# The last query period of a two-branch attention kernel: normalised and turned in two halves, two output tiles' direct sums started earlier, a late GpSimd unit refused

## The chip, the cores and the metric

One core of one Trainium2 chip runs the kernel. The metric is the device time of one execution in microseconds (us), median of several. The profile is one execution, and its span (first to last instruction) is about 1.8 us shorter than that execution's time.

The **time** and the ratio of times say what a user gets. The **aligned distance** says where it comes from: up to a point shortly before the end all kernels here issue the same work, so I count from the start of the exponential with which ScalarE begins its last 14 sets (823.32 us in the profile of the kernel before, 825.29 in that of the changed one) to an event of the closing sequence. In the expectations of the first four runs the count starts 0.3 us later, at the set of score matmuls where the plans part, so 0.3 has to be added to their figures.

## The reference, cut to what matters

```python
g = sigmoid((x * gate_w).sum(-1, keepdims=True))
a = A_ref(x, A_wqkv, A_wo)      # full attention, 32 heads of 16, 2048 tokens, then @ wo
b = B_ref(x, B_wqkv, B_wo)      # sliding dilated attention, window 8, dilation 2, then @ wo
return g * a + (1 - g) * b
```

Both branches end in a 512x512 output projection. The kernel sums the two projections in one bank of PSUM (the memory that matmuls write to) for each tile of 128 tokens: four row blocks of A's `wo` and four of B's.

## The kernel before

The full attention is cut into 32 periods: 512 queries by 4 heads, 64 score tiles of 128 keys each. The exponential of a tile is done by ScalarE (two or three tiles at a time, through the PSUM "ring"), by VectorE (four passes) or by GpSimd (after a copy by VectorE). A tile that an engine takes is called a unit, and the two or three that ScalarE takes at a time a set. Products with V are added into one PSUM bank, `acc`. A planner in the kernel's Python simulates the engines with fixed durations and so fixes the order of instructions on each engine; the chip then follows that order, waiting on semaphores. After the last period comes the closing sequence, and at the very end a closing barrier, in which all engines meet before the program ends. The parts that the change touches:

```python
# which engine gets a score tile
if psc[0] is not None and rem(p) >= PMIN and P.free_at("psc", now):   # PMIN = 20: GpSimd
    hs = P.take("psc", now)
# ...
# after a period: evict acc, transpose, denominator, reciprocal, normalise
if p == NP - 1:
    st["s"] = work.tile([128, QW], FP32, name="accS", tag="accS", bufs=2)
    yield ("act", -1, 0.40, lambda: A.copy(out=st["s"][:, 0:256], in_=acc[:, 0:256]))
    yield ("dve", 0, 0.42, lambda: V.tensor_copy(out=st["s"][:, 256:QW], in_=acc[:, 256:QW]))
# ...
# last period: turn all four tiles back on the PE, one copy, then one matmul per output tile
def tr(s):
    P.thin = 0.05
    w.open(s, [128, QW], BF16)
    for tt in range(TPC):
        PE.transpose(out=w.t[:, tt * 128:(tt + 1) * 128], in_=otok_tiles[c_][:, cb, tt, :], identity=ident[:])
yield ("pe", 8, 0.37, tr, w.kind)
def cp():
    V.tensor_copy(out=oT_tiles[c_][:, cb, :], in_=w.t[:])
yield ("dve", 8, 0.34, cp)
# ...
# output tiles: 0 and 1 have their sum parked in SBUF, 2 and 3 sum directly in a PSUM bank
def direct_job(tt):
    # ... waits for the other row blocks
    w = Bank("e")                       # banks that are free once the ring is
    # ... seven matmuls of the direct sum
    yield ("wait", ev_ot.setdefault((c_, DC - 1), Event()))
    yield ("pe", tt, MM + SW, lambda: mm(w.t[:], oT_tiles[c_][:, DC - 1, tt * 128:(tt + 1) * 128],
                                         awo[:, DC - 1, :], False, True))
    # ... evicted by ScalarE, stored by ScalarE's queue
```

## Time and profile before

| | before |
|---|---|
| time, median of 3 | 852.29 us (852.24 to 852.29) |
| span of the profile, mean granted clock | 849.9 us, 0.999 |
| ScalarE, VectorE, PE, GpSimd busy | 97%, 90%, 89%, 86% |
| end of the last exponential | 839.40 |
| accumulator closed (end of the last matmul into `acc`) | 840.48 |
| last eviction ends, last store issued | 846.18, 846.21 |
| sync engine wakes as the stores have landed | 848.80 |

A row of the page's groups reads: line, engine, operation, output from input, shapes, count, then busy time and mean, then idle time ahead of it and what ended that. The line is a helper's throughout (L347), so one goes by tile names: `ring` scores, `pT` ScalarE's exponentials, `pd` those of VectorE and GpSimd, `acc` the accumulator, `accS` its copy, `otok` the normalised queries, `oT` the same turned, `osb`/`osc` output tiles. ScalarE bounds the kernel until its last exponential. After that only the closing sequence runs, and every part of the change lies in it or just ahead of it. The lines are shown in the prediction.

### The profile page before, as it was taken

Reading aid. Unit: us, or ns where it says so; the run is one execution under the profiler, and the core shown is the slowest. Engines: PE = TensorE matmul, PEld = TensorE weight load, DVE = VectorE, ACT = ScalarE, POOL = GpSimd, SP = SyncE. Lnnn points to the kernel's source line nnn. Section 1 sums busy time; section 2 is a strip of 40 time slices with the busy share of each in tenths; the row PEclk is TensorE's granted clock in tenths of the full one; section 3 lists DMA queues with packets and bytes.
Section 4 is the critical chain, followed back from the end, with each engine's and each line's share of the span. In section 5 each row is a group of like instructions: output and inputs, shape, how many; then the busy total and the mean of one; then the engine's idle time right before and its main releaser. Section 6 shows DMA issues by size and latency. Waiting matters only on the chain.

```text
span 849.9 us, 15786 instructions
## 1 busy us (share of the span) xinstructions
PE 756.6 (89%) x5867; PEld 267.2 (31%) x5867; DVE 763.3 (90%) x1325; ACT 826.4 (97%) x748; POOL 730.8 (86%) x740
## 2 busy tenths in 40 slices
PE   9999999989998888888998988888898898888886
PEld 4432343333323332323323232332223233223222
DVE  5698889899999899998999899999999999999894
ACT  5999999999999999999999999999999999999995
POOL 2596886999799999899999999999899999987783
PEclk9999999999999999999999999999999999999999
DMA  9002304421345140303122413220313230201000
GB/s 294 6 14 88 99 27 140 152 64 41 127 119 162 34 130 24 112 20 99 41 86 75 137 27 124 67 72 12 101 37 108 87 88 20 62 14 57 14 1 26
DMA packets 72590, 63.85 MB, mean 75 GB/s; under 512 B 20528, under 2 KB 69168, under 8 KB 72512
## 3 DMA queue, kind: packets, MB, share of 16 engines
q1 hardware_dynamic: 71168, 62.44, 24.2%
q8 instruction: 46, 0.75, 0.4%
q10 hardware_dynamic: 1344, 0.39, 0.2%
q14 instruction: 32, 0.26, 0.1%
HBM read 46.14 MB, written 12.62 MB: 69 GB/s over the span
## 4 chain that ended last, share of the span: by engine, by line
ACT 66%; issue 20%; PE 11%; DMA 1%; DVE 1%; SPq 0%; ACTq 0%
ACT pT L347 65%; PE w L347 4%; PE ring L347 3%; PE acc L347 3%; ACT lg L347 1%; DMA xr<-in_A_x_dram 1%; PE e L347 1%; DVE ta L347 0%; PE s L347 0%; SPq L347 0%; DVE pd L347 0%; DVE qpk L347 0%; ACT osc L347 0%; DVE osb L347 0%; DVE kvs L347 0%
## 5 line engine op out<-in xcount | busy, mean ns | idle before, releaser
L347 ACT ACTIVATE pT<-ring 128x1536 bf16<-128x1536 f32 x717 | 816.5, 1408 | 6.7 <-PE ring L347 3.7
L347 PE MATMUL ring<-qt,kt_all 32*128 32x512 bf16 x1841 | 284.9, 380 | 83.1 <-ACT pT L347 70.9
L347 DVE SCALAR_TENSOR_TENSOR ta<-ta,w 128x512 f32<-128x512 f32 x474 | 315.7, 681 | 5.6
L347 POOL TENSOR_TENSOR prod<-prod 128x512 f32<-128x512 f32 (+1 forms) x208 | 240.2, 1166 | 5.5
L347 PE MATMUL acc<-pT,vp_all 128*17 128x512 bf16 x1793 | 221.7, 383 | 1.8 <-DVE accS L347 0.9
L347 PEld LDWEIGHTS <-kt_all 32*128 32x128 bf16 x2096 | 112.8, 91 | 336.3 <-issue 326.2
L347 PE MATMUL acc<-ident,z 128*17 128x512 bf16 (+5 forms) x776 | 198.1, 341 | 1.4 <-POOL ident masks.py:199 1.4
L347 DVE TENSOR_SCALAR ta<-w 128x512 f32<-128x512 uint16 x237 | 161.8, 686 | 36.7 <-PE w L347 34.5
L347 DVE SCALAR_TENSOR_TENSOR pd<-ta,w 128x512 uint16<-128x512 f32 x237 | 159.3, 678 | 2.5
L347 POOL TENSOR_TENSOR prod<-ksh,qb 128x512 f32<-128x512 bf16 x128 | 144.7, 1155 | 2.2
L347 POOL TENSOR_TENSOR prod<-vsh,lg 128x512 f32<-128x512 bf16 x128 | 136.7, 1098 | 3.2 <-DMA vsh<-kv_scr 0.8
L347 PE MATMUL w<-qt,kt_all 32*128 32x512 bf16 x255 | 95.4, 383 | 0.0
L347 PE MATMUL acc<-pd,vp_all 128*17 128x512 bf16 x255 | 83.1, 380 | 0.0
L347 PEld LDWEIGHTS <-z 128*17 128x17 bf16 (+1 forms) x783 | 54.2, 91 | 72.1 <-issue 43.4
L347 PEld LDWEIGHTS <-vp_all 128*17 128x17 bf16 x2048 | 40.7, 87 | 90.8 <-issue 90.3
L347 POOL TENSOR_TENSOR psc<-psc 128x512 f32<-128x512 f32 x54 | 64.4, 1193 | 4.2
L347 PE MATMUL w<-bw,xT 128*128 128x512 bf16 x192 | 49.7, 381 | 0.4
L347 POOL TENSOR_SCALAR psc<-psc 128x512 f32<-128x512 uint16 (+1 forms) x36 | 22.2, 618 | 31.6 <-DVE psc L347 29.1
L347 PEld LDWEIGHTS <-xT 128*128 128x128 bf16 x448 | 31.7, 97 | 28.9 <-issue 16.4
L347 POOL TENSOR_TENSOR lg<-lg,mx 128x256 f32<-128x256 f32 x16 | 10.1, 629 | 21.0 <-DVE mx L347 20.8
L347 DVE COPY accS<-acc 128x512 f32<-128x512 f32 (+1 forms) x32 | 21.6, 674 | 5.3 <-ACT accS L347 5.2
L347 DVE CAST kvs<-w 128x512 bf16<-128x512 f32 x32 | 21.9, 684 | 0.9 <-PE w L347 0.8
(108 smaller groups left out, 453.3 us busy)
## 6 DMA issues: line engine op xcount, KB each, us to landing
ksh<-kv_scr SPq DMA_DIRECT2D x16, 1024.0 KB
vsh<-kv_scr SPq DMA_DIRECT2D x16, 1024.0 KB
kv_scr<-kvs SPq DMA_DIRECT2D x16, 256.0 KB
kt_all<-k_scr SPq DMA_DIRECT2D x6, 512.0 KB
q_scr<-qpk SPq DMA_DIRECT2D x24, 128.0 KB
qt<-q_scr SPq DMA_DIRECT2D x24, 128.0 KB
out_dram<-osb SPq DMA_DIRECT2D x14, 128.0 KB
xr<-in_A_x_dram SPq DMA_DIRECT2D x3, 512.0 KB
```

Of the source, the lines that this page charges most:

```text
L347: return chain_on(self._key, f(*a, **k))
```

## The change

Its intent is to shorten the closing sequence. Cut to its core:

```diff
+    PEND = 32
-            if psc[0] is not None and rem(p) >= PMIN and P.free_at("psc", now):
+            if psc[0] is not None and rem(p) >= (PMIN if p < NP - 1 else PEND) and P.free_at("psc", now):
 ...
         P.spent = True
+        yield ("set", ev_spent)                     # the last score set has been issued
 ...
-            yield ("act", -1, 0.40, lambda: A.copy(out=st["s"][:, 0:256], in_=acc[:, 0:256]))
-            yield ("dve", 0, 0.42, lambda: V.tensor_copy(out=st["s"][:, 256:QW], in_=acc[:, 256:QW]))
+            for hf in range(2):
+                cols = slice(256 * hf, 256 * (hf + 1))
+                yield ("dve", 0, 0.36, lambda: V.tensor_copy(out=st["s"][:, cols], in_=acc[:, cols]))
+                yield ("spawn", last_half(st["s"], hf))
+            return
 ...
+    def last_half(src, hf):    # two tiles: transpose, denominator, reciprocal, normalise, turn back;
+        ...                    # half 0 is copied to oT by ScalarE, half 1 by VectorE
+        yield ("set", ev_last[hf])
 ...  direct_job
-        w = Bank("e")
+        yield ("wait", ev_spent)
+        w = Bank()                                  # the two spare banks, free before the ring is
-        yield ("wait", ev_ot.setdefault((c_, DC - 1), Event()))
+        yield ("wait", ev_last[tt // 2])
 ...
-        yield ("act", 0, 0.06, lambda: A.dma_start(...))
+        if tt < TPC - 1:
+            yield ("spawn", dma_job(lambda: SP.dma_start(...)))   # tile 1 now goes out on sync's queue
+        else:
+            yield ("act", 0, 0.06, lambda: A.dma_start(...))
 ...
-            if c_ == NC - 1 and tt >= 2:            # direct sums: tiles 2 and 3
+            if c_ == NC - 1 and tt % 2 == 1:        # now one in each half: tiles 1 and 3
```

Three parts, then: the **refusal** of the late GpSimd unit, the **early sums**, and the **halves** (with which the choice of tiles and the queue of tile 1's store go).

More of the change, by code (lines that the diff above doesn't have):

```diff
@@ L524 @@
     ev_kdone = Event()
+    ev_spent = Event()
+    ev_last = [Event() for _ in range(2)]
     ev_wq = Event()
@@ L1190, in post_job @@
             st["s"] = work.tile([128, QW], FP32, name="accS", tag="accS", bufs=2)
-            yield ("act", -1, 0.40, lambda: A.copy(out=st["s"][:, 0:256], in_=acc[:, 0:256]))
-            yield ("dve", 0, 0.42, lambda: V.tensor_copy(out=st["s"][:, 256:QW], in_=acc[:, 256:QW]))
-        else:
-            yield ("dve", 0, VP, cp)
+            for hf in range(2):
[3 more added lines that the diff above has]
+            return
+        yield ("dve", 0, VP, cp)
         yield ("set", ev_acc[p + 1])
         yield ("wait", ev_g)
-        w = Bank("e" if p == NP - 1 else "w")
+        w = Bank()
         def tr(s):
@@ L1229, in post_job, with tr, den, nrm @@
             yield ("spawn", ot_job(c_, i // 2))
+    def last_half(src, hf):
+        c_, i = periods[NP - 1]
+        tts = range(2 * hf, 2 * hf + 2)
+        w = Bank("e")
+        st = {}
+        def tr(s):
+            w.open(s, [128, 2, 4, 32])
+            for z, tt in enumerate(tts):
+                PE.transpose(out=w.t[:, z].rearrange("p h d -> p (h d)"), in_=src[:, tt * 128:(tt + 1) * 128],
+                             identity=identf[:])
+        yield ("pe", hf, 0.33, tr, "e")
+        def den():
+            st["r"] = work.tile([128, TPC, 4], FP32, name="rden", tag="rden", bufs=2)
+            db = d1[:, c_ * TPC + 2 * hf:c_ * TPC + 2 * hf + 2]
+            V.tensor_tensor(out=st["r"][:, 0:2], in0=w.t[:, :, :, DH],
+                            in1=_ap(db, [list(db.ap[0]), [1, 2], [0, 4]]), op=ALU.mult)
+        yield ("dve", 1 + hf, 0.11, den)
+        yield ("dve", 1 + hf, 0.14, lambda: V.reciprocal(out=st["r"][:, 0:2], in_=st["r"][:, 0:2]))
+        def nrm():
+            r = st["r"]
+            V.tensor_tensor(out=otok_tiles[c_][:, i // 2, 2 * hf:2 * hf + 2, 64 * (i % 2):64 * (i % 2) + 64]
+                            .rearrange("p t (h d) -> p t h d", d=DH),
+                            in0=w.t[:, :, :, 0:DH], in1=_ap(r[:], [list(r[:].ap[0]), [4, 2], [1, 4], [0, DH]]),
+                            op=ALU.mult)
+        yield ("dve", 1 + hf, 0.24, nrm)
+        yield w.close()
+        w2 = Bank("e")
+        def back(s):
+            P.thin = 0.03
+            w2.open(s, [128, 256], BF16)
+            for z, tt in enumerate(tts):
+                PE.transpose(out=w2.t[:, z * 128:(z + 1) * 128], in_=otok_tiles[c_][:, DC - 1, tt, :],
+                             identity=ident[:])
+        yield ("pe", hf, 0.22, back, "e")
+        dst = oT_tiles[c_][:, DC - 1, 256 * hf:256 * (hf + 1)]
+        if hf == 0:
+            yield ("act", 0, 0.40, lambda: A.copy(out=dst, in_=w2.t[:]))
+        else:
+            yield ("dve", 0, 0.22, lambda: V.tensor_copy(out=dst, in_=w2.t[:]))
+        yield w2.close()
+        yield ("set", ev_last[hf])
     def ot_job(c_, cb):
@@ L1233, in ot_job, with turn @@
             yield ("wait", ev_final[c_ - 2])
-        ev = ev_ot.setdefault((c_, cb), Event())
-        if c_ < NC - 1 or cb < DC - 1:
-            def turn():
-                if c_ not in oT_tiles:
-                    oT_tiles[c_] = work.tile([128, DC, QW], BF16, name="oT", tag="oT", bufs=2)
-                SP.dma_start_transpose(out=oT_tiles[c_][:, cb, :].rearrange("p (t n) -> p t n", n=128),
-                                       in_=otok_tiles[c_][:, cb].rearrange("p t d -> p (t d)"))
-            yield ("sp", 0, 0.1, turn)
-            yield ("delay", TURN)
-            if cb == DC - 1:
-                yield ("set", ev_turned[c_])
-            yield ("set", ev)
-            return
-        w = Bank("e")
-        def tr(s):
-            P.thin = 0.05
-            w.open(s, [128, QW], BF16)
-            for tt in range(TPC):
-                PE.transpose(out=w.t[:, tt * 128:(tt + 1) * 128], in_=otok_tiles[c_][:, cb, tt, :],
-                             identity=ident[:])
-        yield ("pe", 8, 0.37, tr, w.kind)
-        def cp():
-            V.tensor_copy(out=oT_tiles[c_][:, cb, :], in_=w.t[:])
-        yield ("dve", 8, 0.34, cp)
-        yield w.close()
-        yield ("set", ev)
+        def turn():
+            if c_ not in oT_tiles:
+                oT_tiles[c_] = work.tile([128, DC, QW], BF16, name="oT", tag="oT", bufs=2)
+            SP.dma_start_transpose(out=oT_tiles[c_][:, cb, :].rearrange("p (t n) -> p t n", n=128),
+                                   in_=otok_tiles[c_][:, cb].rearrange("p t d -> p (t d)"))
+        yield ("sp", 0, 0.1, turn)
+        yield ("delay", TURN)
+        if cb == DC - 1:
+            yield ("set", ev_turned[c_])
+        yield ("set", ev_ot.setdefault((c_, cb), Event()))
     fpart = {}
@@ L1315, in direct_job @@
         yield ("wait", ev_obt[t])
-        w = Bank("e")
+        yield ("wait", ev_spent)
+        w = Bank()
         srcs = [(oT_tiles[c_][:, cb, tt * 128:(tt + 1) * 128], awo[:, cb, :]) for cb in range(DC - 1)]
@@ L1326, in direct_job @@
         for z in range(len(srcs)):
-            yield ("pe", 20 + tt + z / 10, MM + 0.02, pe(z)) + (("e",) if z == 0 else ())
-        yield ("wait", ev_ot.setdefault((c_, DC - 1), Event()))
+            yield ("pe", 20 + tt + z / 10, MM + 0.02, pe(z)) + (("w",) if z == 0 else ())
+        yield ("wait", ev_last[tt // 2])
         yield ("pe", tt, MM + SW, lambda: mm(w.t[:], oT_tiles[c_][:, DC - 1, tt * 128:(tt + 1) * 128],
@@ L1337, in direct_job @@
         yield w.close()
-        yield ("act", 0, 0.06, lambda: A.dma_start(out=out2d[t * 128:(t + 1) * 128, :], in_=st["o"][:]))
+        if tt < TPC - 1:
+            yield ("spawn", dma_job(lambda: SP.dma_start(out=out2d[t * 128:(t + 1) * 128, :], in_=st["o"][:])))
+        else:
+            yield ("act", 0, 0.06, lambda: A.dma_start(out=out2d[t * 128:(t + 1) * 128, :], in_=st["o"][:]))
     def out_steps(t, w, add, prio):
```

## The prediction

> **What bounds the kernel now.** I read the page first, for the engine that sets the length, then the chain of waits over the last 35 us, then the timeline of the last 12 us, because the diff touches only the last of the 32 periods. Busy times and the chain by line:
>
> ```profile
> PE 756.6 (89%) x5867; PEld 267.2 (31%) x5867; DVE 763.3 (90%) x1325; ACT 826.4 (97%) x748; POOL 730.8 (86%) x740
> ACT 66%; issue 20%; PE 11%; DMA 1%; DVE 1%; SPq 0%; ACTq 0%
> L347 ACT ACTIVATE pT<-ring 128x1536 bf16<-128x1536 f32 x717 | 816.5, 1408 | 6.7 <-PE ring L347 3.7
> ```
>
> ScalarE is busy 97% of an 849.9 us span, nearly all in the exponentials, and waits only 6.7 us ahead of them. So until its last exponential ends, only fewer ScalarE units or a shorter end can help. The rest is the end. The chain of waits in order of time (start, length, what) shows it:
>
> ```profile
> 837.69 1.72 ACT pT L347
> 839.41 0.04 issue
> 839.45 0.39 PE acc L347 x3
> 839.84 0.32 PE e L347
> 840.17 0.31 PE acc L347
> 840.48 3.26 PE e L347 x19
> 843.74 0.02 issue
> 843.77 0.43 DVE oT L347
> 844.20 0.05 issue
> 844.25 0.83 PE e L347 x3
> ...
> 845.59 0.59 ACT osc L347
> ```
>
> The last exponential ends at 839.41; nothing but the closing sequence follows, so 849.9 - 839.4 = 10.5 us are serial. Its VectorE side on the timeline (start, length, operation, idle before it and what ended that):
>
> ```profile
> 834.48 1.28 DVE L347 SCALAR_TENSOR_TENSOR pd<-ta,w 128x512 uint16<-128x512 f32 x2
> 840.92 0.42 DVE L347 COPY accS<-acc 128x256 f32<-128x256 f32 x1 [5.17 <-ACT accS L347]
> 842.36 0.17 DVE L347 TENSOR_TENSOR rden<-e,d 128x16 f32<-128x16 f32 x1 [1.01 <-PE e L347]
> 842.56 0.25 DVE L347 RECIPROCAL rden<-rden 128x16 f32<-128x16 f32 x1
> 842.85 0.42 DVE L347 TENSOR_TENSOR otok<-e,rden 128x256 bf16<-128x256 f32 x1
> 843.77 0.42 DVE L347 COPY oT<-e 128x512 bf16<-128x512 bf16 x1 [0.49 <-PE e L347]
> 844.68 1.29 DVE L347 TENSOR_TENSOR osb<-e,fpart 128x512 bf16<-128x512 f32 x2 [0.48 <-PE e L347]
> ```
>
> Each step works on all 512 queries, and waits for the step before: evict, transpose, denominator, reciprocal, normalise, turn back, copy, one matmul per output tile, evict, store. Three losses stand out. The VectorE half of the eviction did not run beside the ScalarE half (840.52 to 840.89) but 0.03 us after it. The last addition into the accumulator (840.17 in the chain, one GpSimd unit's product) comes 0.64 us after the ScalarE units' last, and one matmul of a direct sum went ahead of it. And the transposes of the evicted sums start at 841.72, 0.38 us after the eviction ended at 841.34, behind matmuls of the direct sums.
>
> **What the Trainium skill says.** "PSUM — Partial Sum Buffer", section "PSUM bank collisions raise a hardware error", says that two engines may not be in one bank and quadrant at once, reads included, so software must keep them in turn. The trace agrees: the two half copies read one accumulator and ran one after the other, so splitting by engine gained nothing. "Perfetto Trace Analysis", section "Optimizing Scalar/DVE Operations", says that where VectorE and ScalarE cause bubbles elsewhere, breaking up instructions may let work finish sooner, at about 125 ns of fixed cost for VectorE on PSUM. Here a 512-column copy from PSUM takes 0.68 and a 256-column one 0.42, so the part that does not shrink is 0.16 us in the recorded duration: near that figure. "DMA: Bandwidth & Descriptors", section "Issuing engines are not separate DMA queues", says that stores from different engines share the same 16 DMA engines and only issue time is saved. The four last stores (512 KB) agree: they drain as one burst at about 340 GB/s, some 1.6 us.
>
> **The change, part by part.**
>
> *No late GpSimd unit.* In the last period a GpSimd unit may now be started only with 32 or more units left, not 20. Counting from the timeline, the three score tiles sent to GpSimd near the end are copied by VectorE at 815.13, 824.17 and 828.69. At the last one's score matmul (828.17) there remain sets of 2, 3, 2, 3, 2, 3, 2 and 3 units and three lone units: 23. At the one before (823.65) the same count gives 36. So exactly one unit is refused. That takes 0.64 us (840.48 - 839.84) off the accumulator's end. The unit must go elsewhere. VectorE ends its units at 835.76 and then idles 5.17 us; without the copy it has 0.6 us more, and it may take a unit as long as 7 are left. A unit costs it four passes at 0.6 = 2.4 us. If it takes this one, ScalarE's end stays at 839.4; if ScalarE takes it, its end moves by about a third of a three-unit set's 1.33 us cadence = 0.44 us, and the gain is 0.2 us. I choose 0.45 us, VectorE being the likelier.
>
> *Direct sums in the spare banks.* Both tiles with a direct sum (7 matmuls each, 14 x 0.213 = 3.0 us) may start once the last score set is issued (about 837.6) instead of once the ring banks are free (839.4). The PE has 838.95 to 839.45 idle and fillers before it, so I estimate five or six run there in place of idling. The rest fill waits behind the eviction. Worth up to the 0.38 us at the transposes, but rounding to whole matmuls of 0.21 us leaves some of it.
>
> *Two halves.* I lay out the new tail from the accumulator's end as zero, with durations of the trace above; for half-size steps I take 0.13 us off per 128 fewer fp32 columns. All of these are estimates. VectorE copies half 0 from 0.04 to 0.46 and half 1 to 0.82 (0.36 apart). Half 0: two fp32 transposes 0.52 to 0.90 and, with one direct matmul in the way, 1.0; denominator, reciprocal and normalise (0.20 + 0.29 + 0.29) to about 1.8; turn back 0.25 to 2.1; ScalarE copy 0.37 to 2.5; first output matmul at 2.55. Half 1 is transposed at 1.3, and its three VectorE steps interleave with half 0's: normalised near 2.25, turned at 2.55, copied by VectorE at 2.9, output matmuls 2.95 to 3.6. Two VectorE evictions (0.68 each, 0.60 apart) and two ScalarE ones (0.58, 0.48 apart) then end at about 4.3. On record before: last eviction ended at 846.18 - 840.48 = 5.70. That is 1.4 us shorter. I keep 1.2 us, because order on each engine is fixed by the plan and an eviction of half 0 can stand ahead of half 1's copy. From the last eviction to the end of the span there were 3.7 us (store issue, transfer, completion, closing barrier), and I leave them: three stores instead of two now go out on the sync queue, but spread over as long.
>
> *Added work.* Eight extra small VectorE and PE instructions of 0.2 to 0.3 us lie beside each other's waits; no DMA byte is added.
>
> Sum: 0.45 + 1.2 = 1.65 us of 852.29, that is 0.2%. Before the period's last 22 us nothing in the plan differs, so the other 828 us stay.
>
> **Rivals.**
>
> *ScalarE takes the unit over*: its chain is the bound until 839.4, and every unit it gets is 0.44 us longer. For: VectorE may have only two units in flight and needs 7 left. Against: VectorE's 5 us of idle before the end. It would make 850.9.
>
> *VectorE becomes the bound of the closing sequence*: twice the small instructions, plus half of the accumulator eviction that ScalarE had, plus two of four output evictions. Its sum in the tail is about 0.36 x 2 + 2 x 0.78 + 0.3 + 1.28 = 3.9 us of a 4.3 us sequence, so it has little slack; a badly ordered eviction (0.6) or a late last VectorE unit, now with its product as the accumulator's last, would give about 851.4. Against it: the other half's steps fill latencies.
>
> *The transfer hides it*: if the stores were bound by bandwidth, earlier evictions would only queue. Against: the burst lasts 1.6 us, and 2.6 us pass between the last issue (846.21) and the waiting queue's release (848.80), mostly latency. So a shift of issue shifts the end. If half of it stayed, 851.2.
>
> *Both parts do best*: 0.64 + 1.4 + some of the transfer overlapped, 850.1.
>
> **Range and chances.** I predict 850.6 us. The rivals lie between 850.1 and 851.4, and a timing on another chip can differ by some tenths, as the profiled run's 851.67 beside 852.29 shows. So 849.7 to 851.7 should hold it 8 times in 10. Two per cent would be 17 us, more than the whole 10.5 us closing sequence; faster by that is impossible by this reading, and slower only if the plan were upset earlier. Chances: faster 0.005, same 0.985, slower 0.01.
>
> **What would show it.** In the changed profile: GpSimd's last product ends near 830.2 rather than 836.75; no addition into the accumulator after ScalarE's last set by more than 0.4 us; that end at 839.4 (VectorE took the unit) or 839.85 (ScalarE did); direct-sum matmuls between 837.6 and 839.4; VectorE's second half copy 0.36 us behind its first; the first ScalarE output eviction while half 1 is still being turned; and last store issue near 844.4 to 844.8 instead of 846.21. I am wrong if the transposes of half 0 wait for half 1's copy, if VectorE's late unit ends the accumulator, or if the last eviction is a VectorE one that queued behind others.

## The result, and the profile after

The changed kernel took 850.9 us (median of 4, 850.31 to 852.05), the kernel before 852.29 (852.24 to 852.98) beside it; the ratio is 0.9983, interval 0.9966 to 1.0001. A second set later gave 851.05 against 852.59 and 0.9980 (0.9965 to 0.9995). The first interval just includes 1.

The first look at the two profiles misleads: the changed kernel's span is 850.3 us, longer than the 849.9 before. The cause lies far from the change. The windows view (window, length, busy time of PE, PE loads, VectorE, ScalarE, GpSimd with counts, granted clock, DMA share, GB/s) of the same two stretches, kernel before:

```profile
334.30:337.70 3.40, 2.79 (x23) 1.01 (x23) 2.50 (x7) 3.38 (x4) 3.32 (x4) 1.00 0.02 5
771.20:774.60 3.40, 2.89 (x21) 0.99 (x20) 2.93 (x6) 3.40 (x5) 3.40 (x4) 1.00 0.01 2
```

and changed kernel:

```profile
334.30:337.70 3.40, 3.40 (x21) 1.14 (x17) 2.65 (x6) 2.31 (x3) 3.32 (x4) 0.54 0.01 5
771.20:774.60 3.40, 3.40 (x24) 0.91 (x23) 2.06 (x6) 2.96 (x4) 3.05 (x4) 0.54 0.04 14
```

In this execution the PE twice ran at half clock for 3.41 us. ScalarE, short of scores, was busy for 2.31 instead of 3.38 us in the first. Set against the kernel before, exponential by exponential, it falls back by 1.1 us there and by 0.8 in the second, although the instructions there are the same. The other three executions had mean granted clocks of 0.997 to 1.000, and the one at 1.000 took 850.31 us. That is why I align. "TensorE: Matmul & The Clock Gate", section "What's actually happening", in the Trainium skill, gives the gate two settings and a window of 3413 ns; the stretches here lasted 3.413 us.

Aligned, the changed kernel is 1.6 us shorter: 26.57 us from the chosen exponential to the end before, 24.98 after. The page's counts first, for what went where (changed kernel; before it was x474 and x237):

```profile
L347 DVE SCALAR_TENSOR_TENSOR ta<-ta,w 128x512 f32<-128x512 f32 x476 | 317.1, 681 | 5.6
L347 DVE TENSOR_SCALAR ta<-w 128x512 f32<-128x512 uint16 x238 | 162.5, 686 | 37.9 <-PE w L347 35.8
```

VectorE did 238 units and not 237, ScalarE 717 exponentials as before, GpSimd one unit less: VectorE took the refused unit. ScalarE's timeline, from the chosen exponential to its last store (start, length, operation, count, idle before it):

```profile
825.29 16.07 ACT L347 ACTIVATE pT<-ring 128x1024 bf16<-128x1024 f32 x14
844.23 0.37 ACT L347 COPY oT<-e 128x256 bf16<-128x256 bf16 x1 [2.87 <-PE e L347]
845.30 1.15 ACT L347 CAST osc<-w 128x512 bf16<-128x512 f32 x2 [0.70 <-PE w L347]
846.47 0.37 ACTq L347 DMA_DIRECT2D out_dram<-osc  x1
```

The 14 sets take 16.07 us; before they took 16.08. So nothing was won or lost up to the last exponential. The closing sequence on VectorE, changed kernel:

```profile
842.15 0.76 DVE L347 COPY accS<-acc 128x256 f32<-128x256 f32 x2 [2.74 <-PE acc L347]
843.12 0.17 DVE L347 TENSOR_TENSOR rden<-e,d 128x8 f32<-128x8 f32 x1 [0.22 <-PE e L347]
843.32 0.20 DVE L347 RECIPROCAL rden<-rden 128x8 f32<-128x8 f32 x1
843.56 0.29 DVE L347 TENSOR_TENSOR otok<-e,rden 128x128 bf16<-128x128 f32 x1
843.77 0.15 DVE L347 TENSOR_TENSOR rden<-e,d 128x8 f32<-128x8 f32 x1
843.96 0.20 DVE L347 RECIPROCAL rden<-rden 128x8 f32<-128x8 f32 x1
844.20 0.29 DVE L347 TENSOR_TENSOR otok<-e,rden 128x128 bf16<-128x128 f32 x1
844.87 0.29 DVE L347 COPY oT<-e 128x256 bf16<-128x256 bf16 x1 [0.38 <-PE e L347]
845.08 1.29 DVE L347 TENSOR_TENSOR osb<-e,fpart 128x512 bf16<-128x512 f32 x2
```

Read it against the prediction's lines: the waits of 1.01, 0.49 and 0.48 us between the steps have shrunk to 0.22, 0.38 and none, because the other half's steps stand in them. The two copies together take 0.76 us.

### The profile page after: what moved, and what is told of

The parts are those of the page before. It is cut to its first block, busy times and chain, and to the rows that moved or that the text cites. A ratio compares the mean times of both kernels' runs of the same rounds, so it can differ in the third digit from the quotient of the medians.

```text
span 850.3 us, 15781 instructions
## 1 busy us (share of the span) xinstructions
PE 759.3 (89%) x5864; PEld 267.2 (31%) x5864; DVE 765.4 (90%) x1332; ACT 826.5 (97%) x748; POOL 726.2 (85%) x734
## 4 chain that ended last, share of the span: by engine, by line
ACT 65%; issue 21%; PE 13%; DVE 1%; POOL 0%; ACTq 0%; POOLq 0%
ACT pT L347 64%; PE w L347 5%; PE ring L347 4%; PE acc L347 3%; ACT lg L347 1%; PE s L347 1%; DVE ta L347 0%; PE e L347 0%; DVE pd L347 0%; DVE qpk L347 0%; DVE kvs L347 0%; DVE osb L347 0%; ACT osc L347 0%; ACT e L347 0%; DVE mx L347 0%
## 5 line engine op out<-in xcount | busy, mean ns | idle before, releaser
L347 POOL TENSOR_TENSOR psc<-psc 128x512 f32<-128x512 f32 x51 | 60.9, 1195 | 3.9
```

Source lines behind the costliest of these rows:

```text
L347: return chain_on(self._key, f(*a, **k))
```

## The experiments

Each kernel here was correct, and each has one profile. I cut its closing sequence at two events: the accumulator closed, and sync's first closing wait that ends with a landed store (from the raw records; the views of busy time don't list semaphore instructions). The columns are the aligned time of the first, the two further stretches, and their sum, all in us. The last two columns are the median time with that of the kernel before in the same rounds, and the ratio of means.

| kernel | acc closed | to stores landed | to the end | aligned end | time (before) | ratio |
|---|---|---|---|---|---|---|
| before | 17.16 | 8.32 | 1.09 | 26.57 | | |
| refusal alone (gps_only) | 16.72 | 8.38 | 1.43 | 26.54 | 852.23 (852.59) | 0.9992 |
| early sums alone (spare_only) | 16.88 | 8.33 | 1.09 | 26.29 | 853.2 (852.59) | 1.0000 |
| refusal + early sums (gps_spare) | 16.84 | 8.35 | 1.43 | 26.62 | 852.47 (851.81) | 1.0004 |
| halves alone (halves_only) | 17.15 | 7.11 | 1.09 | 25.35 | 850.92 (852.59) | 0.9978 |
| halves + refusal (halves_gps) | 16.71 | 7.32 | 1.44 | 25.48 | 851.89 (852.58) | 0.9991 |
| halves + early sums (halves_spare) | 16.87 | 6.77 | 1.08 | 24.72 | 850.9 (852.58) | 0.9974 |
| changed kernel, first profile | 16.82 | 6.72 | 1.44 | 24.98 | 850.9 (852.29) | 0.9983 |
| changed kernel again (after_again) | 16.82 | 6.77 | 1.43 | 25.03 | 851.05 (852.59) | 0.9980 |
| changed + GpSimd filling (gp_pad) | 16.82 | 6.92 | 1.09 | 24.84 | 850.68 (852.58) | 0.9974 |
| changed, one unit from VectorE to ScalarE (act_takes_unit) | 17.19 | 6.78 | 1.43 | 25.40 | 851.37 (852.58) | 0.9980 |
| changed, tile 1 stored by ScalarE (store_act) | 16.84 | 7.01 | 1.44 | 25.29 | 851.79 (851.81) | 0.9995 |
| changed, last product added early (pd_early) | 16.73 | 6.81 | 1.44 | 24.98 | 850.87 (851.81) | 0.9991 |
| attempt at a better one (best) | 16.52 | 7.34 | 1.08 | 24.95 | 851.07 (851.81) | 0.9988 |

Rounding leaves 0.01 in some sums. The interval of a ratio is about plus or minus 0.0015, as wide as the whole effect, so the ratios can tell some kernels with the halves from the kernel before, and no two kernels with the halves from each other.

### The three parts, each alone

The diffs are cut to the lines that matter; `...` marks a cut.

The refusal alone, put into the kernel before:

```diff
+    PEND = 32
-            if psc[0] is not None and rem(p) >= PMIN and P.free_at("psc", now):
+            if psc[0] is not None and rem(p) >= (PMIN if p < NP - 1 else PEND) and P.free_at("psc", now):
```

> The kernel before with the refusal of the late GpSimd unit alone. I measure from the set of three score matmuls at which the plans part (823.63 us in the profile before, 825.59 in the changed one) to three points: end of the last exponential (15.77 before, 15.77 changed), end of the last addition into the accumulator (16.85, 16.52), end of the span (26.26, 24.71). Theory (the unit moves to VectorE, and the accumulator closes earlier): 15.77, 16.5, 25.9. Rival (ScalarE takes the unit): 16.2, 16.7, 26.1. Rival (the closing sequence waits for something else, such as the direct sums): 15.77, 16.5, 26.26.

Measured: exponentials 16.08, accumulator 16.72, end 26.54. The accumulator did close 0.44 us earlier and ScalarE did not take the unit, as the theory has it, but the end hardly moved. The loss is in the last two stretches: 0.06 ahead of the landing and 0.34 behind it, in the closing barrier, where the change has no instruction. In the expectation's count the end is 26.23, the number of my last rival (26.26), but that rival put the loss on the direct sums, and so is right by luck. None of my three accounts had the barrier.

The early sums alone, put into the kernel before:

```diff
         P.spent = True
+        yield ("set", ev_spent)
 ...
+        yield ("wait", ev_spent)
-        w = Bank("e")
+        w = Bank()
 ...
```

> The kernel before with the early direct sums alone. Same three distances. Theory (matmuls of the direct sums no longer stand ahead of the transposes): 15.77, 16.85, 25.9. Rival (they still do, because only five or six of fourteen fit in before): 15.77, 16.85, 26.2.

Measured: accumulator 16.88, stretch to landing 8.33. Both were wrong about where the time goes: in the expectation's count the end is 25.98, near the theory's 25.9, but that is luck. The gain I expected at the transposes did not come; a gain of 0.28 came at the accumulator instead. The PE's timeline of this kernel shows both (start, length, operation, count):

```profile
841.89 0.39 PE L347 MATMUL acc<-pT,vp_all 128*17 128x512 bf16 x3
842.12 0.38 PE L347 MATMUL acc<-pd,vp_all 128*17 128x512 bf16 x1
842.43 1.47 PE L347 MATMUL w<-bwo,obt 128*128 128x512 bf16 x6
843.73 0.60 PE L347 MATMUL e<-identf,accS 128*128 128x128 f32 x4
```

GpSimd's late product (`pd`) now follows ScalarE's last set directly. In the kernel before a matmul of a direct sum stood between them. And six matmuls of the sums still stand between the accumulator and the transposes, which start 1.24 us after it, in all four kernels without the halves. The planner places the transposes where it believes the eviction to be done: its own durations for the two copies and their latencies add up to 0.40 + 0.22 + 0.42 + 0.12 = 1.16 us. With halves it reckons 0.36 + 0.12 = 0.48 for the first, and the transposes start at 0.59. That the sums stand there because of these figures is argued from the code, not tested.

The halves alone are the changed kernel with the other two parts undone:

```diff
-    PEND = 32
+    PEND = 20
 ...
-        yield ("wait", ev_spent)
-        w = Bank()
+        w = Bank("e")
 ...
```

> The changed kernel with both other parts undone, so the two halves alone. Theory (the chain of whole-tile steps was what made the tail long): 15.77, 16.85, 25.4, a tail after the accumulator of 8.5 instead of 9.41. Rival (direct sums on the PE fill the tail, so halves alone wait behind them): 26.0 or more.

Measured: accumulator 17.15, end 25.35. In the expectation's count that is 16.84 and 25.04, a tail of 8.20: the rival (26.0 or more) is out, and the gain is 0.36 larger than the theory's 25.4. This part alone gives 1.22 of the change's 1.59 us.

And the changed kernel, with no edit, on the same chip:

> The changed kernel again on the chip of these runs. 15.77, 16.52, 24.71 as in its first profile; its span differs from that only by how many stretches of half clock fall into it.

Measured: 25.03 from the exponential, against 24.98 in the first profile (the expectation's 24.71 counts from the later point). So 0.05 is what one repeat shows, and the 850.8 us of its span had one half-clock stretch in it.

### The parts in pairs

Refusal and early sums without the halves, that is, the first two edits above together in the kernel before:

> The kernel before with the refusal and the early sums but without the halves; the last corner of the three parts. Counted from the exponential at 823.32 in the profile before. Theory (refusal and early sums each get the same third of a microsecond at the accumulator, and the refusal costs 0.3 in the closing barrier): accumulator 16.82, tail 9.7, end 26.5, about the 26.57 of before. Rival (the two add): accumulator 16.5, end 26.2 or less.

Measured: 16.84, 9.79 behind it, end 26.62. The theory holds: the two do not add at the accumulator, 16.72 and 16.88 alone and 16.84 together. With early sums the PE is still at a sum when ScalarE's last set is ready (in the changed kernel 0.15 us pass between the exponential's end at 841.36 and the set's first matmul, before it was 0.05), and that eats part of the refusal's gain. The early sums also have nothing left to remove there: with the refusal alone the last product (839.69) already follows ScalarE's last set (839.48) with no sum between them.

Halves and refusal, that is, the changed kernel with the direct sums back in the later banks:

```diff
-        yield ("wait", ev_spent)
-        w = Bank()
+        w = Bank("e")
 ...
```

> The changed kernel without the early direct sums. Theory (the sums and the refusal are two ways to the same 0.3 to 0.4 us at the accumulator; without early sums the last ScalarE eviction is late, as in the run with halves alone): accumulator 16.75, tail 8.5, end 25.2. Rival (early sums matter on top): end 25.4 or more.

Measured: 16.71, stretch to landing 7.32, end 25.48. The rival is nearer: with the halves the early sums matter, 0.60 us to the landing beside the refusal and 0.34 without it, though they gave nothing there in the whole-tile sequence. ScalarE's timeline of the kernel with the halves alone shows why:

```profile
842.55 0.37 ACT L347 COPY oT<-e 128x256 bf16<-128x256 bf16 x1 [3.19 <-PE e L347]
843.74 0.59 ACT L347 CAST osc<-e 128x512 bf16<-128x512 f32 x1 [0.82 <-PE e L347]
845.17 0.59 ACT L347 CAST osc<-e 128x512 bf16<-128x512 f32 x1 [0.84 <-PE e L347]
```

The second output eviction (`osc`) comes 1.43 us after the first, because matmuls of its tile's direct sum still had to run after the turned half was ready. In the changed kernel the two follow each other at once (one line of 1.15 us for both). A faster chain only pays if what runs in its gaps has been moved out as well.

Halves and early sums, that is, the changed kernel without the refusal:

```diff
-    PEND = 32
+    PEND = 20
```

> The changed kernel with the late GpSimd unit allowed again. Counted from the same exponential: accumulator closed at 16.85 as with the early sums alone (16.88; changed 16.82), tail 7.9 with the fast barrier. Theory (refusing the unit gains nothing once the sums are early, and costs 0.29 in the barrier): end at 24.75, so 0.2 to 0.3 shorter than the changed kernel. Rival (the refusal is worth what the prediction gave it): accumulator at 17.15, end at 25.3.

Measured: accumulator 16.87, then 6.77 and 1.08, end 24.72. The theory's 24.75 is confirmed. **Without the refusal the kernel ends 0.26 to 0.31 us earlier than the changed one.** Across the four pairs that differ in the refusal alone, it moves the end by -0.03, +0.33, +0.13 and +0.26 us: never a gain that the repeatability lets one claim.

### What the refusal costs in the barrier

In the closing barrier GpSimd first takes two steps. Its records in the profile before, in the changed kernel and in the kernel of the next experiment (start, length, instruction):

```
before    849.22 0.02 EVENT_SEMAPHORE    849.30 0.02 EVENT_SEMAPHORE    849.39 0.08 DRAIN
changed   849.25 0.02 EVENT_SEMAPHORE    849.62 0.02 EVENT_SEMAPHORE    849.71 0.14 DRAIN
gp_pad    848.05 0.02 EVENT_SEMAPHORE    848.14 0.02 EVENT_SEMAPHORE    848.22 0.08 DRAIN
```

With the late unit the trace has an 8 KB fetch of instructions at about 830 us, while GpSimd works. Without the unit, in the changed kernel, that fetch starts only at 850.60, after the span's end at 850.27. The test gives GpSimd its instruction count back:

```diff
         yield ("set", ev_spent)
+        for _ in range(7):
+            yield ("pool", 0, 0.1, lambda: G.memset(gpad[:], 0.0))
```

> The changed kernel with seven GpSimd clears of one unused column at the end of its work, while GpSimd idles, so that its instruction count is again about that of the kernel before. Seen so far: in the closing barrier GpSimd takes 0.37 us between its two steps in the three profiles without the late unit, and 0.08 in the three with it, and an instruction fetch of 8 KB moves from 830 us to beside the barrier. Theory (GpSimd's instructions run into an unfetched block in the barrier): the step is back to 0.08, the tail after the accumulator 7.87 instead of 8.16 to 8.21, from the parting point to the end 24.7 instead of 25.0 (counted from the exponential at 823.32 in the profile before). Rival (the step depends on what GpSimd did long before, idle time for one): 0.37 and 8.2 as in the changed kernel.

(The expectation's "beside the barrier" is not exact: see below.) Measured: the step is 0.08 again, the fetch is back at 830.67, and the last stretch is 1.09 instead of 1.43 to 1.44. The stores landed 0.15 to 0.20 later than in the changed kernel, although they were issued at the same times after the accumulator, which I cannot explain, so the end came out at 24.84 and not 24.7. The stretch itself leaves no doubt: over all 14 profiles it is 1.08 or 1.09 in the six where GpSimd has the unit or the filling, and 1.43 or 1.44 in the eight where it has neither. GpSimd has 849 instructions of all kinds in each of the six and 842 in each of the eight. The filling takes 1.03 us, the unit's six compute instructions about 5.5. So the cost hangs on how many instructions GpSimd has, not on what they do. That the step waits for the late fetch, as the theory has it, does not fit: in all eight profiles the fetch starts after the span's end, 0.7 to 1.0 us after the slow step is over (850.60 against 849.62 in the changed kernel). What the step waits for is open. "Runtime: NRT & Kernel Launch", section "Instruction fetch mechanics", in the Trainium skill, calls the cost of crossing a block mostly hidden; whether the 0.35 us here are such a crossing, no run shows.

The page has it in sight, if one knows where. The waits of the sync queue in the closing part, kernel before:

```profile
SPq L1652 <- DMA out_dram<-osc: 2.5, 1, 2.5
SPq L1652 <- PEq L1652: 0.6, 2, 0.4
```

changed kernel:

```profile
SPq L1692 <- DMA out_dram<-osb: 1.7, 1, 1.7
SPq L1692 <- PEq L1692: 0.9, 2, 0.5
```

gp_pad:

```profile
SPq L1695 <- DMA out_dram<-osb: 1.8, 1, 1.8
SPq L1695 <- PEq L1695: 0.6, 2, 0.4
```

The barrier's wait is put down to the PE's sequencer, which came last in it, but it goes from 0.6 to 0.9 and back with GpSimd's instruction count.

### The price of the first rival

```diff
-    DV_END = 7
+    DV_END = 12
```

> The changed kernel with VectorE's units of the last period ending when 12 are left, not 7: VectorE takes one unit less and ScalarE one more (one more exponential of one tile, 718 in all). This prices the prediction's first rival. Theory: the last exponential ends 0.44 to 0.5 later, at 16.55; the accumulator at 17.0; end 25.2. If the exponential ends later and the accumulator does not, the price was on VectorE's late product instead.

Measured (from the start of the last 15 sets, since there is one more): 718 exponentials, the last one ending at 16.56, so 0.49 later, as expected; the accumulator at 17.19 and the end at 25.40, 0.37 to 0.42 later than the changed kernel and 0.2 later than the theory's 17.0 and 25.2. So one unit costs 0.4 us if ScalarE takes it, and the prediction's choice of VectorE was both right and worth that much.

### Three attempts to gain more

Tile 1's store from ScalarE's queue again:

```diff
-        if tt < TPC - 1:
-            yield ("spawn", dma_job(lambda: SP.dma_start(...)))
-        else:
-            yield ("act", 0, 0.06, lambda: A.dma_start(...))
+        yield ("act", 0, 0.06, lambda: A.dma_start(...))
```

> The changed kernel with tile 1's store issued by ScalarE again, so sync issues two stores and ScalarE two. In the changed profile the last store is issued by sync at 4.61 after the accumulator, 0.35 after its data were ready at 4.26, since sync takes about 0.45 for each store. Theory (serial issue on the sync queue sets the end): last issue at 4.4, tail shorter by 0.2, 7.95 to 8.0. Rival (the four stores drain as one burst and the last issue does not matter, as the run with halves alone suggests, where the last issue came 0.7 later and the tail only 0.3 later, the barrier taken out): tail 8.1 to 8.2.

Measured: the last issue did come 0.25 us earlier (4.36 after the accumulator instead of 4.61), yet the stores landed at 7.01, later than in any of the other kernels with halves, early sums and the same last issue (6.72 to 6.92). The tail is 8.45, above both accounts, so both fail; but 7.01 is only 0.09 above the latest of four profiles that themselves spread by 0.2, and this is one profile. By the packet records its last packet ends at 6.50, among the 6.37 to 6.55 of those four; what is longer is the time from there to the waking, 0.5 and not 0.35 us. Between last issue and landing there were 2.40 to 2.65 us in the five kernels with two stores on each queue and evictions close together, and 1.76 to 2.32 in all others, but those others also differ in when the stores start. Why is open.

VectorE's last product added as soon as it is ready:

```diff
-        if act_left[p] == 0:
+        if act_left[p] == 0 or (p == NP - 1 and rem(p) <= 3):
             yield ("spawn", pv_job(p, [(t, j, st["pd"][:])], ("pd", ds), 0.9, False))
```

> The changed kernel with VectorE's last product added by a matmul of its own as soon as it is ready, not behind ScalarE's last set. It was ready at 839.4 in the changed profile and added at 841.73, 0.22 after the set's three. Theory: accumulator 0.22 earlier, 16.6; the rest as in the changed kernel, end 24.75 to 24.8. Rival (the matmul pushes something else on the PE, since the order is fixed): accumulator 16.8.

Measured: accumulator 16.73, end 24.98. The gain of 0.22 was halved at once, since ScalarE's last set then waited behind a sum on the PE, and what was left was lost in a later eviction of tile 3 (it began at 3.96 after the accumulator, not 3.75). The rival was right in kind.

The combination: halves and early sums, the late unit allowed, its product planned earlier, tile 1 on ScalarE's queue.

```diff
-    PEND = 32
+    PEND = 20
-        yield ("delay", SLACK)
-        if act_left[p] == 0:
+        yield ("delay", SLACK if p < NP - 1 else 0.8)
+        if act_left[p] == 0 or (p == NP - 1 and rem(p) <= 3):
 ...                                                # tile 1's store from ScalarE, as above
```

> Halves and early sums with the late GpSimd unit allowed (so the fast barrier), that unit's product added ahead of ScalarE's last set instead of behind it, and tile 1's store from ScalarE. Theory (the savings add): accumulator 16.65, tail 7.7 to 7.85, end 24.4 to 24.5, some 0.5 less than the changed kernel and 2.1 less than before; time about 850.2 where the kernel before has 852.3. Rival (GpSimd's product is not ready in time and the PE waits for it): accumulator 17 or more.

Measured: the accumulator at 16.52, the earliest of all, but the end at 24.95. ScalarE's last eviction began 4.85 us after the accumulator instead of 3.75, and the stores landed at 7.34. A matmul of tile 3's sum did come behind the turned halves, but the last matmul ended at 845.20, 0.84 before the eviction began, so it explains little of this. The rest is on ScalarE, which issued tile 1's store between its two evictions (845.21 to 845.57) and then waited, by the profile, for VectorE's last output tile:

```profile
846.04 0.58 ACT L347 CAST osc<-w 128x512 bf16<-128x512 f32 x1 [0.87 <-DVE osb L347]
```

Why it waits for that is not shown. The savings did not add. By aligned distance the best kernel is the changed one without the refusal (24.72); its time, 850.9 us and 0.9974 of the kernel before, cannot be told from the changed kernel's 0.9980 to 0.9983.

## Why the prediction was right or wrong

It gave 850.6 us in a range of 849.7 to 851.7 and "within 2%"; 850.9 and 851.05 were measured. Step by step:

- **What bounds, and nothing before the last 22 us changes**: right. The 14 last sets take 16.07 us against 16.08, and ScalarE still does 717 exponentials. The prediction did not see that half-clock stretches move an execution by 1 to 2 us; its allowance for another chip covered them by luck.
- **One unit refused, VectorE takes it**: right in both; 238 units on VectorE. The price of the other choice, put at 0.44, was 0.49 at the exponential and about 0.4 at the end.
- **0.45 us for the refusal**: this is the term that failed. Alone it does close the accumulator 0.44 us earlier, as chosen, but it does not add to the early sums. The whole change closes the accumulator 0.34 us earlier, but the early sums alone reach 0.28, and the refusal beside halves and early sums adds 0.05 there. It then costs 0.35 in the barrier, which the prediction held fixed at "3.7 us from the last eviction to the end". Net, the refusal lost about 0.3 us.
- **The early sums relieve the transposes**: wrong. The wait of 0.38 us before the transposes stayed with early sums alone (1.24 us from accumulator to transposes in both), so it was not for these sums to be moved; that it lies in the planned order is argued above, not tested. With the halves the 1.24 became 0.59. Six matmuls did run before the last exponential's end, as estimated, and the worth of the early sums lay elsewhere: at the accumulator, and in letting the halved sequence run free.
- **The halves, 1.4 laid out and 1.2 kept**: the layout was close. Counted from the accumulator, first output matmul 2.55 predicted and 2.55 measured (844.66 - 842.11); second copy 0.34 us behind the first against 0.36; half 1 normalised at 2.38 against 2.25; its output matmuls 3.1 to 3.7 against 2.95 to 3.6; last eviction at 4.33 against 4.3. So it was 1.37 us, and the caution of 0.2 was not needed: half 1's copy stood ahead of half 0's eviction on VectorE. The stores then landed another 0.2 us sooner after the last eviction. This 1.37 is of all three parts together; early sums were in it, since with the halves alone the last eviction began 4.73 us after the accumulator and not 3.75.
- **The sum**: 0.34 at the accumulator + 1.60 to the landing - 0.35 in the barrier = 1.59, against 0.45 + 1.2 = 1.65. The total agrees more closely than its terms; the halves paid for what the refusal gave back.
- **Rivals**: VectorE as bound of the closing sequence did not come true. From its first copy (842.15) to its last eviction (846.37) it idles 0.6 us ahead of its instructions, so it has little slack, as said, but nothing queued badly. That the transfer hides the gain did not come true either: the landing moved 1.60 us for a last eviction moved by 1.37 and a last issue moved by 1.12 (5.73 to 4.61). The raw packet records say where the 1.60 lies: the first packet of the four stores starts 1.23 us earlier after the accumulator (4.53 and not 5.76), as the first issue does, and first to last packet takes 1.84 us and not 2.16. So neither "mostly latency" fits (in the profile before these packets run from 846.24 to 848.40, most of the 2.6 us between last issue and waking), nor does the last issue alone set the end.
- **The signs it named**: one of its three signs of being wrong came true, and the total hides it. VectorE's last product does end the accumulator, as the changed kernel's PE timeline shows:

```profile
841.51 0.39 PE L347 MATMUL acc<-pT,vp_all 128*17 128x512 bf16 x3
841.73 0.38 PE L347 MATMUL acc<-pd,vp_all 128*17 128x512 bf16 x1
```

  It was ready at 839.41, and the plan put it 0.22 us behind the set; `pd_early` shows that taking it away gains nothing at the end. ScalarE's first output eviction (845.30) also did not start while half 1 was being turned, but after half 1's copy (844.87 to 845.16). And "ends near 830.2" for GpSimd's last product is a slip: 830.19 is where that instruction starts, and it ends at 830.81. The last issue at 21.43 us from the exponential, 844.75 in the count of the profile before, lay in the range named.

## What to carry to other kernels

A serial end, where each engine waits for the one before, is shortened by cutting the data so that the pieces fill each other's waits; count the gain from the waits in the timeline, and move out whatever work had been hiding in them, or it becomes the new wait. Test the parts of a bundled change alone and in pairs: here one of three gained nothing at the end and cost a third of a microsecond in a place that it does not touch. Where executions differ by more than the effect, align two profiles at the last point at which their work is the same, and measure from there.

## What the Trainium skill lacked or had wrong

- "Runtime: NRT & Kernel Launch", section "Instruction fetch mechanics", calls the cost of a block boundary mostly hidden and speaks of 16 KiB blocks. The kernels whose GpSimd has six or seven compute instructions fewer lost 0.35 us in the closing barrier (1.43 to 1.44 us from landing to end in eight profiles, 1.08 to 1.09 in the six others), and there are instruction fetches of 8 KB beside those of 16 KB. Whether a block boundary is the cause is open.
- No page says what splitting the last stores over two issuing queues does to their landing. "DMA: Bandwidth & Descriptors", section "Issuing engines are not separate DMA queues", lets one expect only issue time to change; with two stores on each queue instead of three and one, they were issued 0.25 us sooner and landed 0.1 to 0.3 us later (7.01 against 6.72 to 6.92 us after the accumulator). One profile of it, near the spread of 0.2, cause open.
- "Perfetto Trace Analysis", section "Optimizing Scalar/DVE Operations", is borne out in that breaking up instructions let the work finish sooner. It puts the fixed part of a VectorE instruction on PSUM at about 125 ns, and at about twice that in profiled duration. Here copies and products take 0.68, 0.42 and 0.29 us for 512, 256 and 128 fp32 columns, so the part that does not shrink is 2 x 0.42 - 0.68 = 0.16 us of profiled duration, less than the doubled figure. The smallest steps hardly shrink: the denominator takes 0.17 us for 16 columns and 0.15 to 0.17 for 8, the reciprocal 0.25 and 0.20.
- "TensorE: Matmul & The Clock Gate", section "A second HAM failure mode: psum-queue depth-cycling", explains a clock that falls back within steady work by frequent short idle times of the PE. Here single windows of 3.413 us at half clock came in some executions of a kernel whose PE is 89% busy, and cost 1.1 and 0.8 us in the changed kernel's first profile. The page gives no way to tell when such a window falls: just ahead of the first (330.60 to 334.00) the PE was busy for 2.58 us in the changed kernel, and for the same 2.58 us in the kernel before, where the clock stayed full.
